# Channel attention into a rational feed-forward layer: a new table of times for the planner, batch 0's sums and the weight conversion on VectorE, the softmax division folded into the split of the fused weights, and three of eight denominators as a product

## The chip, the cores and the metric

The kernel runs on one core of a Trainium2 chip. The time is that of one launch in device microseconds, the median of a few runs. The profile shows one further execution by engine: PE is TensorE (matrix products), DVE is VectorE, ACT is ScalarE, POOL is GpSimd, and SP is SyncE, which here issues every DMA.

## What is computed

```python
# attention over channels, for each of B = 4 batches; q, k, v are [6080, 256]
qn = q / (norm(q, axis=tokens) + 1e-6);  kn = k / (norm(k, axis=tokens) + 1e-6)
s  = kn.T @ qn / tau                       # 256 x 256
a  = exp(s - s.max(-1));  a /= a.sum(-1) + 1e-9
x  = v @ a                                 # 6080 x 256
# a feed-forward layer with a rational activation, over all 24320 tokens
h  = x @ w_in                              # 256 -> 2048
P  = a0 + a1*h + a2*h**2 + a3*h**3
Q  = 1 + abs(b0)*abs(h) + abs(b1)*h**2
out = (P / (Q + 1e-6)) @ w_out             # 2048 -> 256
```

All arrays are float32, except that w_in and w_out reach the kernel as pairs of 32-bit words (float64), from which it forms float32 itself.

## The kernel before

**Tiles and loops.** Tokens are taken in groups of 512 (`GT`); 12 groups make a batch, the last with 448 tokens. The 2048 hidden channels are taken in eight *pairs* of 2 x 128 channels. A pair (`pair`) works on a tile of 128 x 1024 numbers: 12 matmuls fill it in PSUM (`mm1`, into a buffer `hx`), the activation is computed on it, and 8 matmuls by w_out add it to the group's output `acc` (`mm2`, in two steps). In the trace an f32 matmul leaves two records, so `mm2` has 16 records for a pair and `mm1`, in another number format, has 12.

**Attention ahead of time.** `x @ w_in` is not computed in two steps. For each batch, `Attn` streams q and k (24 halves of a group, a buffer `kq` each), lets PE add up k.T @ q, and squares both on ACT (`sq`) for the norms. `softmax` turns this into `ex`, `shares` divides it by its sums (`inverse`), `turned` transposes it into `eT`, and `fuse` multiplies it by w_in: PE writes a tile, ACT copies it to a rounded part `whi`, and DVE forms the rest `wlo`. So `mm1` needs only v: `values` transposes a group of v on PE (into `hx`), and splits it in the same way into `vhi` and `vlo`. Batch b+1's attention runs under batch b's pairs; that of batch 0 stands at the start of the program with nothing to run under.

**Weights.** `piece` makes float32 of 16 pieces (8 of w_in, 8 of w_out), each with an Abs on ACT, five DVE instructions (`low_bits`, `high_bits`, `power`, `low_word`, `cut_off`) and an addition on POOL (`together`).

**A pair's activation.** ACT: Square(h) into `d`, Abs(b0*h) into `kk`, a3*h+a2 into `y`, Abs_reciprocal_sqrt of `d` into `r`, and its Square. POOL: `d = b1*d + 1`, `d += kk`, and later `d = d*r` for one step that refines the quotient. DVE: two steps of P's Horner scheme in `hx`, its product with `r`, and the last step, which writes `g`, the operand of `mm2`.

**What sets the order.** Every piece of work is a `step` with an engine, a cost and a key. The `Planner` plays the steps through with these costs and hands out buffers; on each engine it picks the ready step with the lowest key. The order that comes out is written down, and every engine then runs its instructions strictly in that order. `SLOTS` gives the buffers of each kind: three `hx` (PSUM) are shared by the pairs' tiles, the scores, the transposes and the fused weights, so an `hx` comes free only when its last reader, mostly DVE's last step of a pair, is done. There are also four `d`, four `g`, three `r` and two `sq`.

Of the kernel before, what the change touches and what calls it, by code (L numbers as in the profile page):

```python
# [16 lines left out]
PSUM = bass.MemoryType.PSUM  # L17

# [32 lines left out]
class Step:  # L51
    __slots__ = ("eng", "cost", "fn", "key", "need", "after", "new", "bufs", "banks", "n")


class Planner:

# [8 lines left out]
    def add(self, eng, cost, key, fn, reads=(), writes=()):  # L65
        s = Step()
        s.eng, s.cost, s.fn, s.key = eng, cost, fn, key
        s.n = len(self.steps)
        s.after, s.new, s.bufs = [], [], []
# [26 lines left out]
    def order(self):  # L96
# [26 lines left out]
        while left:  # L123
            for e in ready:
                while busy[e] <= now and ready[e]:
# [17 lines left out]
                    busy[e] = now + pick.cost  # L143
                    for b in pick.banks:
                        b.owner, b.until = e, busy[e] + self.HOP[e]
# [23 lines left out]
def tile_channel_attention_rational_ffn(  # L169
# [15 lines left out]
    P = 128  # L185
# [9 lines left out]
    while n0 < N:  # L195
# [7 lines left out]
    LINE = ("POOL",) * NFP  # L203
# [7 lines left out]
    SLOTS = {"hx": 3, "acc": 1, "d": 4, "uu": 4, "r": 3, "g": 4, "w": 5, "kq": 3, "sq": 2, "ssq": 1,  # L211
             "vst": 1, "vhi": 2, "vlo": 2, "orow": 2, "sacc": 1, "eT": 1, "n2": 1,
             "s0": 1, "y": 1, "e": 1, "sm": 1}
    plan = Planner(SLOTS, ("d", "uu", "r", "g", "w", "kq", "sq", "vst", "vhi", "vlo", "orow"), ("hx", "acc"))
# [23 lines left out]
    def step(eng, cost, key, fn, reads=(), writes=()):  # L238
# [7 lines left out]
        plan.add(eng, cost, key, run, reads, writes)  # L246
# [17 lines left out]


    edge = ONE**0.5
    root, incline, fold, t0, t1, t2 = (
        const.tile([P, 1], F32, name=x) for x in ("root", "incline", "fold", "t0", "t1", "t2")
    )
    dve.tensor_scalar_max(t0, b1, 1e-30)  # L270
    act.activation(t1, t0, AF.Abs_reciprocal_sqrt)
    dve.tensor_tensor(root, t0, t1, op=ALU.mult)
    dve.tensor_tensor(t2, root, root, op=ALU.mult)
    dve.tensor_tensor(t2, t0, t2, op=ALU.subtract)
    dve.scalar_tensor_tensor(t2, t2, 0.5, t1, op0=ALU.mult, op1=ALU.mult)
    dve.tensor_tensor(root, root, t2, op=ALU.add)
    dve.scalar_tensor_tensor(incline, root, -2.0 * edge, b0, op0=ALU.mult, op1=ALU.add)
    dve.tensor_scalar_mul(fold, b0, -2.0)

# [5 lines left out]
    II = 3.5  # L285
    T0 = 80.0
# [3 lines left out]
    def piece(side, m, at, late):  # L290
# [7 lines left out]
        raw = buf("d", [P, 2 * PIECE], U32, "raw")  # L298
        keep = buf("uu", [P, PIECE], F32, "keep")
        top = buf("g", [P, PIECE], U32, "top")  # L300
        unit = buf("r", [P, PIECE], U32, "unit")
# [12 lines left out]
        def low_bits():  # L314
            dve.tensor_scalar(top.tile, hi(), 3, 0x3FFFFFF8, op0=ALU.logical_shift_left, op1=ALU.bitwise_and)

        def high_bits():

            dve.scalar_tensor_tensor(
                top.tile, hi(), 0xC0000000, top.tile, op0=ALU.bitwise_and, op1=ALU.bitwise_or  # L320
            )

        def power():
            dve.tensor_scalar(unit.tile, top.tile, 0xFF800000, None, op0=ALU.bitwise_and)
# [22 lines left out]
        step("DVE", 0.75, c + 2, power, [top], [unit])
        step("DVE", 0.7, c + 3, low_word, [raw, unit], [unit])
        step("POOL", 1.3, c + 4, together, [top, unit], [unit])
        if side == "in":  # L350
            step("DVE", 1.4, c + 5, lambda: cut_off(w_in_sb[:, j, cols]), [keep, unit], [w_in_ok[part, j]])
        else:
            dst = w_out_sb[:, 2 * m : 2 * m + 2].rearrange("p f e -> p (f e)")
            step("DVE", 1.1, c + 5, lambda: cut_off(dst), [keep, unit], [w_out_ok[m]])


    class Attn:


        def __init__(self, b, begin, pace, end):  # L360
            self.b = b
            self.ssq = {}
# [3 lines left out]
            for i in range(2 * NG):  # L366
                self.half(i, begin + i * pace, begin + (i + 1 - i % 2) * pace, sps, "POOL" if not first or i % 3 == 2 else "DVE")
# [3 lines left out]
        def half(self, i, at, both, sps, eng):  # L371
# [12 lines left out]
            step("SP", 1.4, at - (0 if first else 2 * II), load, (), [kq])  # L384

            if half == 0:
                self.slot = sps or buf("hx", [P, 2, GT], F32, "sps")
            slot = self.slot

            def products():  # L390
                for t in range(T // 2):
                    for c in range(NC2):
                        pe.matmul(
                            slot[:, 0, c * C : (c + 1) * C],
                            kq[:pn, t, 0, c * P : (c + 1) * P],
                            kq[:pn, t, 1, :],
                            start=(t == 0 and c == 0 and half == 0 and (g == 0 or not first)),
                            stop=(t == T // 2 - 1 and half == 1 and (g == NG - 1 or not first)),
                            skip_group_check=True,
                        )  # L400

            joined = half == 1 or (first and g > 0)
            step("PE", 1.75, both, products, [kq, slot] if joined else [kq], [slot])
            if half == 1 and not first:
# [7 lines left out]
            if eng not in self.ssq:  # L412
                sq = self.ssq[eng] = buf("orow" if eng == "DVE" else "ssq", [P, 2 * 2 * C], F32, "ssq")
                step("ACT", 1.05, at, lambda: act.activation(sq[:pn], src[1](), AF.Square), [kq], [sq])
            else:
                sq, total = buf("sq", [P, 2 * 2 * C], F32), self.ssq[eng]
                step("ACT", 1.05, at, lambda: act.activation(sq[:pn], src[1](), AF.Square), [kq], [sq])
                e = pool if eng == "POOL" else dve
                step(
                    eng, 2.42 if eng == "POOL" else 1.4, at + 2,  # L420
                    lambda: e.tensor_tensor(total[:pn], sq[:pn], total[:pn], op=ALU.add), [sq, total], [total],
                )

        def softmax(self, at):
# [5 lines left out]
            sums = list(self.ssq.values())  # L430

            def norms_pe():
                parts = [(s, h) for s in sums for h in range(T // 2)]
                for n, (s, h) in enumerate(parts):
                    end = n == len(parts) - 1
                    row = s[:, h * 2 * C : (h + 1) * 2 * C]
                    pe.matmul(
                        nps[:, 0, 0:C], ones, row[:, C : 2 * C], start=(n == 0), stop=end, skip_group_check=True
                    )
                    for i in range(NC2):  # L440
                        pe.matmul(
                            nps[:, 0, C + i : C + i + 1], row[:, i * P : (i + 1) * P], ones[:, 0:1],
                            start=False, stop=end, skip_group_check=True,
                        )

            step("PE", 2.0 * len(sums), at, norms_pe, sums, [nps])
# [12 lines left out]
            step("DVE", 6.5, at + 4, norms_y, [n2, s0], [y, e])  # L459
# [29 lines left out]
            step("ACT", 4.0, at + 10, exps, [sn, stat], [ex, stat])  # L489
# [5 lines left out]
            step("DVE", 0.5, at + 12, inverse, [stat], [stat])  # L495

            def shares():
                for i in range(NC2):
                    act.activation(
                        ex[:, i, :], ex[:, i, :], AF.Identity, scale=stat[:, 3 * NC2 + i : 3 * NC2 + i + 1]  # L500
                    )

            step("ACT", 1.0, at + 13, shares, [ex, stat], [ex])
# [10 lines left out]
            step("PE", 0.7, at + 14, turned, [ex], [eps])  # L514
            fn = lambda: act.copy(eT.tile.rearrange("p j i -> p (j i)"), eps[:, 0, :])
            step("ACT", 0.6, at + 13, fn, [eps], [eT])
            self.w = [self.fuse(j, at + 16 + 2 * II * j, eT) for j in range(NFP // 2)]

        def fuse(self, j, at, eT):

            slot = buf("hx", [P, 2, GT], F32, "fused")
            hi = buf("w", [P, 2, NC2, 2 * P], F32R, "whi")
# [142 lines left out]
    for n, m in enumerate(range(8)):  # L665
        piece("in", m, 8.0 + 4.0 * n, 6.0)
# [52 lines left out]
```

## Time and profile before

| | |
|---|---|
| median of 3 runs | 2801.58 us (2799.64 to 2801.61) |
| profiled execution: its time, its span | 2800.71 us, 2798.9 us |
| busy: PE, DVE, ACT, POOL | 96%, 74%, 77%, 87% of the span |
| first `mm1` starts at | 132.41 us |
| first group's output copied at | 213.9 us |
| group of 512 without attention beside it | 50.9 us |
| moved by DMA | 110 MB, 90% of the DMA engines' time in the first 70.6 us |

Times are microseconds from the span's start. A row of the timeline has start, duration, engine, line, operation, output<-inputs with their shapes, and in brackets how long the engine stood idle before it and for whom. Line 30 is the helper through which all instructions are issued, so rows are told apart by their tiles. The rows of a table by stretches have, for each engine, busy time and (x) instructions, then the granted PE clock as a share, the share of DMA time, and GB/s. In the chain of waits a row has start, length, engine and tile, and the number of instructions.

### The profile page before, as it was taken

How to read it: one execution, taken by the hardware profiler on the slowest of the kernel's cores; microseconds unless marked ns; L12 is line 12 of the kernel's file. 1: busy time of each engine (PE TensorE's matmuls, PEld its weight loads, DVE VectorE, ACT ScalarE, POOL GpSimd, SP SyncE). 2: the span in 40 equal slices, each digit the busy share in tenths (PEclk: the TensorE clock that was granted, in tenths of full speed). 3: DMA queues.
4: the chain of work that ended last, by engine and by line, in shares of the span. 5: the costliest groups of instructions: out<-in, count | busy, mean ns of one | idle time of the engine just before them, and what ended most of it. 6: DMA issues, size and time to landing. Idle time of an engine off the chain costs nothing.

```text
span 2798.9 us, 32559 instructions
## 1 busy us (share of the span) xinstructions
PE 2689.2 (96%) x12236; PEld 2280.4 (81%) x12236; DVE 2075.6 (74%) x1800; ACT 2157.4 (77%) x2188; POOL 2432.9 (87%) x1251
## 2 busy tenths in 40 slices
PE   7489999999999999999999999999999999999999
PEld 6468888888788888888878888888887888888887
DVE  7687777777767777777776777777777677777776
ACT  4378888787777878887786787878777788888886
POOL 3489999999779999999887999999896799999997
PEclk9699999999999999999999999999999999999999
DMA  9300111110000101010100111111100000000000
GB/s 289 93 8 31 31 38 44 49 36 29 31 30 31 46 31 61 31 46 30 59 15 15 45 36 56 31 46 34 47 16 16 15 31 16 16 31 16 30 8 15
DMA packets 69326, 110.11 MB, mean 39 GB/s; under 512 B 5296, under 2 KB 53936, under 8 KB 69168
## 3 DMA queue, kind: packets, MB, share of 16 engines
q1 hardware_dynamic: 69168, 108.03, 12.0%
q8 instruction: 96, 1.57, 0.2%
q14 instruction: 62, 0.51, 0.1%
HBM read 83.10 MB, written 24.90 MB: 39 GB/s over the span
## 4 chain that ended last, share of the span: by engine, by line
PE 57%; POOL 22%; ACT 8%; DVE 5%; issue 5%; DMA 1%; SPq 0%; ACTq 0%; POOLq 0%; DVEq 0%
PE acc L30 28%; PE hx L30 28%; POOL d L30 21%; ACT uu L30 3%; ACT r L30 2%; ACT d L30 2%; POOL ssq L30 2%; DVE g L30 2%; DMA kq<-in_q_dram 1%; DVE hx L30 1%; ACT orow L30 0%; DVE w_out_sb L30 0%; DVE sq L30 0%; DVE r L30 0%; DVE y L30 0%
## 5 line engine op out<-in xcount | busy, mean ns | idle before, releaser
L30 PE MATMUL acc<-w_out_sb,g 128*128 128x256 f32 (+1 forms) x6144 | 1384.5, 379 | 9.7 <-ACT orow L30 8.4
L30 PEld LDWEIGHTS acc<-w_out_sb,g 128*128 128x128 f32 (+1 forms) x6144 | 1155.9, 189 | 182.6 <-ACT orow L30 11.7
L30 PE MATMUL hx<-vhi,w 128*128 128x512 f32 (+1 forms) x3072 | 1047.5, 407 | 39.8 <-DVE g L30 32.5
L30 POOL TENSOR_TENSOR d<-d,r 128x1024 f32<-128x1024 f32 (+1 forms) x384 | 903.8, 2360 | 89.4 <-ACT r L30 88.7
L30 POOL TENSOR_TENSOR d<-d,uu 128x1024 f32<-128x1024 f32 (+1 forms) x384 | 908.0, 2365 | 32.2 <-POOL d L30 0.3
L30 DVE TENSOR_TENSOR uu<-uu,hx 128x1024 f32<-128x1024 f32 (+1 forms) x384 | 463.4, 1207 | 392.3 <-ACT uu L30 391.7
L30 PEld LDWEIGHTS hx<-vhi,w 128*128 128x128 f32 x3072 | 581.9, 189 | 179.3 <-DVE g L30 41.2
L30 ACT ACTIVATE d<-hx 128x1024 f32<-128x1024 f32 (+1 forms) x384 | 388.6, 1012 | 295.0 <-PE hx L30 293.9
L30 PE MATMUL hx<-vlo,w 128*128 128x512 f32 (+1 forms) x1536 | 598.9, 390 | 0.0
L30 DVE SCALAR_TENSOR_TENSOR g<-d,hx 128x1024 f32<-128x1024 f32 (+1 forms) x384 | 462.8, 1206 | 154.2 <-POOL d L30 142.5
L30 ACT ACTIVATE r<-d 128x1024 f32<-128x1024 f32 (+1 forms) x384 | 405.6, 1056 | 203.6 <-POOL d L30 201.8
L30 POOL TENSOR_SCALAR d<-d,babs 128x1024 f32<-128x1024 f32 (+1 forms) x384 | 429.4, 1118 | 144.8 <-ACT d L30 144.1
L30 DVE SCALAR_TENSOR_TENSOR hx<-hx,coef,r 128x1024 f32<-128x1024 f32 (+1 forms) x384 | 489.9, 1276 | 76.4 <-ACT r L30 76.2
L30 DVE SCALAR_TENSOR_TENSOR hx<-uu,coef,hx 128x1024 f32<-128x1024 f32 (+1 forms) x384 | 488.6, 1272 | 6.1
L30 ACT ACTIVATE uu<-hx,coef 128x1024 f32<-128x1024 f32 (+1 forms) x384 | 462.2, 1204 | 0.2 <-DVE w_out_sb L30 0.2
L30 ACT ACTIVATE uu<-hx,babs 128x1024 f32<-128x1024 f32 (+1 forms) x384 | 425.0, 1107 | 1.4 <-PE hx L30 1.4
L30 ACT ACTIVATE r<-r 128x1024 f32<-128x1024 f32 (+1 forms) x384 | 406.1, 1057 | 5.0
L30 PEld LDWEIGHTS hx<-vlo,w 128*128 128x128 f32 x1536 | 291.8, 190 | 55.0
L30 POOL TENSOR_TENSOR ssq<-sq,ssq 128x1024 f32<-128x1024 f32 (+1 forms) x76 | 183.7, 2417 | 49.1 <-ACT sq L30 48.4
L30 PE MATMUL hx<-kq 128*128 128x256 f32 (+1 forms) x672 | 157.8, 390 | 11.5 <-DMA kq<-in_q_dram 6.9
L30 PEld LDWEIGHTS hx<-kq 128*128 128x128 f32 (+1 forms) x672 | 130.9, 196 | 32.8 <-DMA kq<-in_k_dram 6.9
L30 ACT ACTIVATE sq<-kq 128x1024 f32<-128x1024 f32 (+1 forms) x79 | 82.4, 1058 | 53.6 <-DMA kq<-in_q_dram 36.4
(71 smaller groups left out, 724.9 us busy)
## 6 DMA issues: line engine op xcount, KB each, us to landing
vst<-in_v_dram SPq DMA_DIRECT2D x44, 512.0 KB, 3.6
out_dram<-orow SPq DMA_DIRECT2D x44, 512.0 KB, 2.7
kq<-in_k_dram SPq DMA_DIRECT2D x78, 256.0 KB, 3.6
kq<-in_q_dram SPq DMA_DIRECT2D x78, 256.0 KB, 4.0
d<-in_moe_w_in_dram SPq DMA_DIRECT2D x8, 512.0 KB, 5.8
d<-in_moe_w_out_dram SPq DMA_DIRECT2D x8, 512.0 KB, 3.6
r<-in_k_dram SPq DMA_DIRECT2D x10, 256.0 KB, 5.7
r<-in_q_dram SPq DMA_DIRECT2D x10, 256.0 KB, 5.9
```

The costliest lines, as they stand in the source:

```text
L30: ins = op(*args, **kwargs)
```

## The change

- Order: `TIME` and `LAG` give the keys of all stages; the start of the pairs has key 52.18 (80 before), and a pair's steps have other distances. The planner also learns that some DVE steps and all POOL steps exclude each other (`port`).
- Start: v's group 1 is loaded only after the first `whi` (`gate`). Batch 0's squares are all summed on DVE (`orow`; before, a third of them went to POOL). Four pieces of w_in are converted early; four others and all of w_out come later, in buffers of their own (`cv`, `cv2`) with their raw words in `kq` (four of them now), and `together` moves from POOL to DVE. A DVE step `fold` halves the sum before the norms' matmuls, of which 3 are left for each batch (before: 12 for batch 0, 6 for the others).
- Softmax: `shares` is gone. `fuse` works on one pair's weights (8 tiles for a batch, before 4 of double size); ACT multiplies by 1/sum while it writes `whi`, as two instructions of 128 x 256, and DVE does so while it writes `wlo`, also as two.
- Attention: both halves of a group are multiplied in one step. Batch 1's 24 halves follow at 0.95 pairs each (before 3.4), those of batches 2 and 3 at 2.7.
- Denominator: from the second group on, pairs 1, 5 and 7 (`FACTORED`) form Q - 1 as h*(b1*abs(h) + b0) with an Abs, a DVE product and another Abs; the one is added as the bias of the root on ACT, and by a POOL instruction for the later product. This has five ACT, five DVE and two POOL instructions, where the other pairs have five, four and three.

```diff
+LAG = {
+    "first": 3.38, "prod": 6.03, "abs": -6.89, "line": 2.25, "second": 4.09, "sum": -5.43, "slope": 5.2,
...
+TIME = {
+    "pair": 3.54, "start": 52.18, "load": 2.03, "softmax": 48.33, "in": 9.33, "late_in": 4.0, "out0": 1.98,
...
-    SLOTS = {"hx": 3, "acc": 1, "d": 4, "uu": 4, "r": 3, "g": 4, "w": 5, "kq": 3, "sq": 2, "ssq": 1,
+    SLOTS = {"hx": 3, "acc": 1, "d": 4, "uu": 4, "r": 3, "g": 4, "w": 10, "kq": 4, "sq": 2, "ssq": 1,
...
-        raw = buf("d", [P, 2 * PIECE], U32, "raw")
+        early = side == "in" and m < 4
+        raw = buf("d" if early else "kq", [P, 2 * PIECE], U32, "raw")
+        work = buf("uu" if early else "cv", [P, 2, PIECE], F32, "work")
+        unit = buf("r" if early else "cv2", [P, PIECE], U32, "unit")
...
-            pool.tensor_tensor(rest, rest, top.tile.bitcast(F32), op=ALU.add)
+            dve.tensor_tensor(rest, rest, top(F32), op=ALU.add)
...
-                e = pool if eng == "POOL" else dve
+                e = dve if first else pool
...
+            def fold():
+                dve.tensor_tensor(total[:, : 2 * C], total[:, : 2 * C], total[:, 2 * C :], op=ALU.add)
...
-                    act.activation(
-                        ex[:, i, :], ex[:, i, :], AF.Identity, scale=stat[:, 3 * NC2 + i : 3 * NC2 + i + 1]
-                    )
...
+                    act.activation(hi[:, i, :], src, AF.Identity, scale=share)
...
+                    dve.scalar_tensor_tensor(
+                        lo[:, i, :], src, share, hi[:, i, :].bitcast(F32), op0=ALU.mult, op1=ALU.subtract
+                    )
...
+        if m >= NFP and p in FACTORED:
+            fn = lambda: act.activation(c(kk), c(hx), AF.Abs, scale=b1)
+            fn = lambda: dve.scalar_tensor_tensor(c(d), c(kk), b0, c(hx), op0=ALU.add, op1=ALU.mult)
+            fn = lambda: act.activation(c(d), c(d), AF.Abs)
...
+        more = ONE if m >= NFP and p in FACTORED else 0.0
+        fn = lambda: act.activation(c(r), c(d), AF.Abs_reciprocal_sqrt, bias=more)
+        if m >= NFP and p in FACTORED:
+            fn = lambda: pool.tensor_scalar(c(d), c(d), ONE, None, op0=ALU.add)
...
+    gate = [attns[0].w[0][0]]
```

**PE between batch 0's norms and the first pair.** Before; `ident,vst` is the transposition of v's group 1, `ident,sq` is `turned`, `w_in_sb,eT` is `fuse`, `kq` is k.T @ q:

```order
L30 MATMUL hx_112<-ones,ssq_121 128x1 x2
L30 MATMUL hx_112<-ident,vst_138 128x128 x8
L30 MATMUL hx_111<-kq_116 128x256 x4
L30 MATMUL hx_111<-kq_114 128x256 x4
L30 MATMUL hx_112<-ident,sq_119 128x128 x4
L30 MATMUL hx_113<-kq_115 128x256 x4
L30 MATMUL hx_111<-w_in_sb,eT_127 128x256 x8
L30 MATMUL hx_112<-w_in_sb,eT_127 128x256 x8
L30 MATMUL hx_113<-kq_116 128x256 x4
L30 MATMUL hx_111<-vhi_139,w_128 128x512
```

Now:

```order
L43 MATMUL hx_101<-ones,orow_102 128x1 x2
L43 MATMUL hx_100<-kq_93 128x256 x4
L43 MATMUL hx_100<-kq_92 128x256 x4
L43 MATMUL hx_101<-ident,sq_105 128x128 x4
L43 MATMUL hx_99<-w_in_sb,eT_111 128x256 x4
L43 MATMUL hx_100<-w_in_sb,eT_111 128x256 x4
L43 MATMUL hx_101<-kq_92 128x256 x4
L43 MATMUL hx_101<-kq_94 128x256 x4
L43 MATMUL hx_99<-vhi_133,w_112 128x512
```

Before, `turned` went into the `hx` in which v's group 1 had just been transposed; now it goes into that of the norms, and v's group 1 comes after the first two pairs.

**DVE at the same place.** Before, the reader of that `hx` (`vlo`) stood here, behind the conversion of w_out:

```order
L30 SCALAR_TENSOR_TENSOR g_105<-d_97,g_105 128x512
L30 SCALAR_TENSOR_TENSOR w_out_sb<-uu_100,r_108 128x512
L30 TENSOR_SCALAR r_109<-g_105 128x512
L30 SCALAR_TENSOR_TENSOR r_109<-d_97,r_109 128x512
L30 TENSOR_TENSOR vlo_142<-hx_112,vhi_140 128x1024
L30 COPY sacc_143<-hx_113 128x512
L30 TENSOR_TENSOR sacc_143<-hx_111,sacc_143 128x512
L30 TENSOR_TENSOR w_133<-hx_111,w_128 128x1024
```

Now the first two `wlo` stand between pieces, and conversions go on between the first group's pairs:

```order
L43 SCALAR_TENSOR_TENSOR w_in_sb<-cv_96,cv_98 128x512
L43 TENSOR_SCALAR cv_97<-kq_93 128x512
L43 SCALAR_TENSOR_TENSOR cv_97<-kq_93,cv_97 128x512
L43 SCALAR_TENSOR_TENSOR w_122<-hx_99,sm_110,w_112 128x256 x2
L43 SCALAR_TENSOR_TENSOR w_123<-hx_100,sm_110,w_113 128x256 x2
L43 TENSOR_SCALAR cv_98<-cv_97 128x512
L43 TENSOR_TENSOR sacc_137<-hx_101,sacc_137 128x512
L43 SCALAR_TENSOR_TENSOR cv_98<-kq_93,cv_98 128x512
```

Before, three pieces of w_out were converted between the softmax and this `vlo`. Now the conversion is spread: 28 of its instructions stand between the second `wlo` and the first group's last `g`.

**POOL in a group without attention.** Before, every pair had three rows:

```order
L30 TENSOR_SCALAR d_97<-d_97,babs 128x1024
L30 TENSOR_TENSOR d_97<-d_97,uu_102 128x1024
L30 TENSOR_TENSOR d_96<-d_96,r_110 128x1024
L30 TENSOR_SCALAR d_99<-d_99,babs 128x1024
L30 TENSOR_TENSOR d_99<-d_99,uu_101 128x1024
L30 TENSOR_TENSOR d_97<-d_97,r_108 128x1024
```

Now a pair of `FACTORED` (here `d_84` and `d_82`) has two, without the addition of `uu`:

```order
L43 TENSOR_SCALAR d_84<-d_84 128x1024
L43 TENSOR_TENSOR d_84<-d_84,r_91 128x1024
L43 TENSOR_SCALAR d_81<-d_81,babs 128x1024
L43 TENSOR_TENSOR d_81<-d_81,uu_85 128x1024
L43 TENSOR_TENSOR d_81<-d_81,r_90 128x1024
L43 TENSOR_SCALAR d_82<-d_82 128x1024
L43 TENSOR_TENSOR d_82<-d_82,r_89 128x1024
```

More of the change, by code (lines that the diff above doesn't have):

```diff
@@ L51 @@
 class Step:
-    __slots__ = ("eng", "cost", "fn", "key", "need", "after", "new", "bufs", "banks", "n")
+    __slots__ = ("eng", "cost", "fn", "key", "need", "after", "new", "bufs", "banks", "port", "n")
 class Planner:
@@ L107, in order @@
         events, out, now = [], [], 0.0
+        port = {"DVE": 0.0, "POOL": 0.0}
         for s in self.steps:
@@ L143, in order @@
                     busy[e] = now + pick.cost
+                    if pick.port:
+                        other = "POOL" if e == "DVE" else "DVE"
+                        busy[e] = max(now, port[other]) + pick.cost
+                        port[e] = busy[e]
                     for b in pick.banks:
@@ L201, in tile_channel_attention_rational_ffn @@
     TG = B * NG
-    LINE = ("POOL",) * NFP
+    FACTORED = (1, 5, 7)
     pe = InOrder(tc, nc.tensor)
@@ L244, in run @@
             fn()
-        plan.add(eng, cost, key, run, reads, writes)
+        plan.add(eng, cost, key, run, reads, writes, port)
     ident = const.tile([P, P], F32, name="ident")
@@ L284, in tile_channel_attention_rational_ffn, with piece @@
     PIECE = 512
-    II = 3.5
-    T0 = 80.0
+    II = TIME["pair"]
+    T0 = TIME["start"]
     w_in_ok = {(part, j): Buf() for part in range(4) for j in range(NC2)}
     w_out_ok = [Buf() for _ in range(NFP)]
-    def piece(side, m, at, late):
+    def piece(side, m, at, c):
         if side == "in":
@@ L366, in __init__, with half @@
             for i in range(2 * NG):
-                self.half(i, begin + i * pace, begin + (i + 1 - i % 2) * pace, sps, "POOL" if not first or i % 3 == 2 else "DVE")
+                both = begin + (i if first else i + 1 - i % 2) * pace
+                self.half(i, begin + i * pace, both, sps)
             self.scores = sps if first else self.sacc
             self.softmax(end)
-        def half(self, i, at, both, sps, eng):
+        def half(self, i, at, both, sps):
             g, half = divmod(i, 2)
@@ L382, in load @@
                     sp.dma_start(kq[:pn, :, j, :], rows[:, half * T // 2 : (half + 1) * T // 2, :])
[L384 to L404, printed above, removed]
+            step("SP", 1.4, at - (0 if first else 2 * II), load, self.gate, [kq])
+            self.kq[half] = kq
+            if first:
+                fn = lambda: self.products(sps, [kq], pn, i == 0, i == 2 * NG - 1)
+                step("PE", 1.75, both, fn, [kq, sps] if i else [kq], [sps])
+            elif half == 1:
+                pair, slot = list(self.kq), buf("hx", [P, 2, GT], F32, "sps")
+                step("PE", 3.5, both, lambda: self.products(slot, pair, pn, True, True), pair, [slot])
                 if g == 0:
@@ L521, in fuse @@
+        def fuse(self, p, at, eT, stat):
             slot = buf("hx", [P, 2, GT], F32, "fused")
[L522 to L535 removed]
@@ new lines, in fuse, with part @@
+            lo = buf("w2", [P, NC2, 2 * P], F32R, "wlo")
+            cols = slice(2 * p * P, 2 * (p + 1) * P)
+            def part(i):
+                return slot[:, 0, i * 256 : (i + 1) * 256], stat[:, 3 * NC2 + i : 3 * NC2 + i + 1]
+            def products():
+                for i in range(NC2):
+                    for c in range(NC2):
+                        pe.matmul(
+                            part(i)[0], eT[:, c, i * P : (i + 1) * P], w_in_sb[:, c, cols],
+                            start=(i == 0 and c == 0), stop=(c == NC2 - 1), skip_group_check=True,
+                        )
```

231 lines of the change are left out of this document (103 added, 128 removed).

## The prediction

> **What bounds the kernel now.** I read the page first, then busy time by stretches (the groups' ends as borders), the chain of waits in a plain group, and the timeline at the start and at a softmax.
>
> ```profile
> span 2798.9 us, 32559 instructions
> PE 2689.2 (96%) x12236; PEld 2280.4 (81%) x12236; DVE 2075.6 (74%) x1800; ACT 2157.4 (77%) x2188; POOL 2432.9 (87%) x1251
> ...
> core 0: us, PE busy (x) PEld busy (x) DVE busy (x) ACT busy (x) POOL busy (x), PEclk, DMA share, GB/s
> 0.00:70.60 70.60, 52.03 (x216) 43.54 (x216) 52.39 (x55) 34.37 (x38) 27.56 (x20) 0.95 0.90 289
> 70.60:132.41 61.81, 26.95 (x101) 22.91 (x101) 45.16 (x59) 18.04 (x24) 29.85 (x17) 0.64 0.28 85
> 132.41:213.90 81.49, 70.53 (x296) 57.88 (x295) 65.85 (x55) 59.51 (x61) 65.81 (x34) 0.94 0.06 20
> 315.70:703.40 387.70, 383.61 (x1754) 325.54 (x1753) 283.95 (x240) 310.63 (x310) 362.52 (x184) 1.00 0.13 41
> 833.60:1384.50 550.90, 543.70 (x2482) 461.11 (x2481) 402.84 (x340) 441.78 (x440) 513.40 (x260) 1.00 0.13 40
> 1384.50:1448.90 64.40, 57.93 (x267) 49.89 (x266) 50.84 (x50) 48.47 (x56) 48.53 (x26) 0.95 0.11 33
> 2346.10:2397.00 50.90, 50.87 (x234) 42.94 (x233) 39.55 (x34) 42.03 (x43) 46.87 (x25) 1.00 0.06 22
> ```
>
> The last row is a group of batch 3, with no attention beside it: PE is busy 50.87 of 50.90 us. That is the floor, and the change does not touch it: a group keeps its matmuls. The chain of waits in such a group is made of PE alone, and gives the price of a pair's `mm1` (12 records) and `mm2` (16 records):
>
> ```profile
> 2342.32 3.45 PE acc L30 x16
> ...
> 2354.78 2.76 PE hx L30 x12
> ```
>
> So a pair costs PE 6.2 us, a record of `mm1` 0.23 us, any other f32 record of 256 columns 0.216 us. What can be won is PE's idle time: the start (until 213.9 us), about 6.5 us at a softmax (row 1384.5; there are three such stretches), and 4.1 + 7.2 + 7.2 us in the groups with attention (rows 315.7, 833.6; the third, in batch 2, repeats the second).
>
> **The start up to the first pair.** Before, the last sum of squares ends on POOL at 70.6 us, and the first `mm1` starts 62 us later:
>
> ```profile
> 67.78 2.83 POOL L30 TENSOR_TENSOR ssq<-sq,ssq 112x1024 f32<-112x1024 f32 x1 [6.03 <-ACT sq L30]
> ...
> 114.31 2.78 POOL L30 TENSOR_TENSOR ssq<-sq,ssq 128x1024 f32<-128x1024 f32 x1
> 114.82 2.82 DVE L30 SCALAR_TENSOR_TENSOR w_out_sb<-uu,r 128x512 f32<-128x512 f32 x1
> ...
> 118.62 1.22 DVE L30 TENSOR_TENSOR vlo<-hx,vhi 128x1024 fp32r<-128x1024 f32 x1
> 119.99 1.09 PE L30 MATMUL hx<-ident,sq 128*128 128x128 f32 x4 [21.88 <-DVE vlo L30]
> ...
> 132.41 0.58 PE L30 MATMUL hx<-vhi,w 128*128 128x512 f32 x1
> ```
>
> PE stands 21.88 us before `turned`, since its `hx` is held until `vlo`, which DVE reaches only behind the conversion; and the conversion is slow, since an instruction between SBUF tiles takes 2.82 us while POOL works, against 0.68 and 0.42 us where POOL is idle:
>
> ```profile
> 9.45 1.23 DVE L30 TENSOR_TENSOR orow<-sq,orow 128x1024 f32<-128x1024 f32 x1 [2.46 <-ACT sq L30]
> 16.24 2.56 DVE L30 TENSOR_SCALAR g<-d 128x512 uint32<-128x512 uint32 x1 [0.39 <-DMA d<-in_moe_w_in_dram]
> 22.97 0.42 DVE L30 TENSOR_SCALAR g<-d 128x512 uint32<-128x512 uint32 x1
> 29.85 0.68 DVE L30 SCALAR_TENSOR_TENSOR w_in_sb<-uu,r 128x512 f32<-128x512 f32 x1
> ```
>
> In the new order POOL has nothing until batch 1's squares, so the sums and pieces run at the short prices. A piece is then 0.42 + 0.68 + 0.42 + 0.68 + 0.62 (`together`, half of 1.23) + 0.68 = 3.5 us. Up to its last sum DVE has 23 sums x 1.23, seven pieces x 3.5 and a `vlo` of 1.22: 54 us, from 9.45 us on, so 63.5 us, and some 4 us of waits at the first loads: 68 us. The loads are not later: 33 transfers of 0.52 MB up to batch 0's last half make 17.3 MB, 60 us at the 289 GB/s of the first stretch; the two w_out and w_in pieces ahead of that half on SP's queue wait for `kq` tiles that DVE frees by 50 us.
>
> From 68 us DVE has, up to the scores' maximum, `fold` 0.6, the norms (2.6 of small steps, 1.9 of reciprocals), the scores 1.7, and 16 instructions of pieces at 9.3: 16 us. Then exps 1.4 and `turned` 1.1 (slow clock), `eT` 0.6, the first weights' 8 records at half speed 3.4, the second's 1.7, four halves of batch 1 at 0.216 x 16 = 3.5 for the two that stand ahead: 12 us. DVE's way to the first `wlo` (13 instructions, 7 us) and its 0.95 us fit under that. First `mm1` at 68 + 28 = 96 us, 36 us earlier. PE's work done by then shrinks: before 64.5 us (24 halves 41.5, six of batch 1 10.4, norms 3.5, transposes 2.2, four weights 6.9), now 54.1 (41.5, four halves 6.9, 0.9, 1.3, two weights 3.5). Of the difference of 10.4, 2.6 are norms that are gone; 8 us come later. **Term: -36 + 8 = -28 us.** Bounds: the sums end at 66 or 72, and POOL's first three additions for batch 1 may stop DVE for up to 3 x 2.4 us: -34 to -17.
>
> The loads of w_out that move behind the start meet idle DMA engines (share 0.28, then 0.06). The new wait, group 1's v behind the first `whi`, lets it land some 4 us later (the row below), while PE has two `mm1` (5.5 us) ahead of its transposition: nothing.
>
> ```profile
> vst<-in_v_dram SPq DMA_DIRECT2D x44, 512.0 KB, 3.6
> ```
>
> **The first group.** Before it lasts 81.5 us for 296 records, about 67.5 us of PE work; 14 us are lost. Now PE has eight pairs' `mm2` 27.6, eleven `mm1` 30.3, six weights 10.4, eight halves 13.8, a transposition 0.9: 83 us. DVE has more:
>
> ```profile
> L30 DVE SCALAR_TENSOR_TENSOR hx<-hx,coef,r 128x1024 f32<-128x1024 f32 x10 | 12.8, 1284 | 1.4 <-ACT r L30 1.4
> L30 DVE SCALAR_TENSOR_TENSOR hx<-uu,coef,hx 128x1024 f32<-128x1024 f32 x10 | 12.8, 1281 | 0.1
> L30 DVE TENSOR_TENSOR uu<-uu,hx 128x1024 f32<-128x1024 f32 x10 | 12.2, 1215 | 12.6 <-ACT uu L30 12.6
> L30 DVE SCALAR_TENSOR_TENSOR g<-d,hx 128x1024 f32<-128x1024 f32 x10 | 12.1, 1213 | 0.3
> L30 DVE SCALAR_TENSOR_TENSOR w_out_sb<-uu,r 128x512 f32<-128x512 f32 x3 | 6.3, 2096 | 1.1 <-POOL r L30 1.1
> ...
> L30 DVE TENSOR_SCALAR r<-g 128x512 uint32<-128x512 uint32 x2 | 3.5, 1733 | 0.0
> ```
>
> These are DVE's groups in 132 to 214 us. Eight pairs x 5.0 = 40; 28 instructions of pieces, 16.6 us at the short prices, and a wait for POOL on each: the eleven of before took 15.8 us instead of 6.5, 0.85 each, so 24 us; seven `wlo` x 0.95, a `vlo`, four additions of scores (0.69): 10. Sum 91 us from about 93 us on, so the last `g` comes at 184 at the earliest, with waits for ACT and POOL near 190, and PE's end of the group near 194: 98 us, of which 15 are lost, as before. **Term: 0.** Bounds: PE alone sets the time (-14), or every one of the 28 waits for a whole POOL instruction of 2.39 us: (2.39 - 0.85) x 28 = +43.
>
> ```profile
> L30 POOL TENSOR_TENSOR d<-d,uu 128x1024 f32<-128x1024 f32 x352 | 840.9, 2389 | 29.6 <-POOL d L30 0.3
> ```
>
> A wait on DVE holds the pairs behind it, and through `g` PE; that is why the price of the lock counts here and nowhere else.
>
> **The three later softmaxes.** Before, DVE works 16.2 us from one `g` to the next, PE waits 6.19 us, and then runs 12 matmuls in 4.5 us that take 2.4 (7/8 of 2.76) elsewhere:
>
> ```profile
> 1416.06 1.22 DVE L30 SCALAR_TENSOR_TENSOR g<-d,hx 128x1024 f32<-128x1024 f32 x1 [0.80 <-POOL d L30]
> ...
> 1426.81 3.56 DVE L30 SCALAR_TENSOR_TENSOR sq<-sacc,n,y 128x256 f32<-128x256 f32 x2
> ...
> 1432.24 1.21 DVE L30 SCALAR_TENSOR_TENSOR g<-d,hx 128x1024 f32<-128x1024 f32 x1
> ...
> 1433.50 0.74 PE L30 MATMUL hx<-vhi,w 128*128 128x448 f32 x1 [6.19 <-DVE g L30]
> ...
> 1434.42 0.95 PE L30 MATMUL hx<-vhi,w 128*128 128x448 f32 x2
> ...
> 153.79 0.50 PE L30 MATMUL hx<-vhi,w 128*128 128x512 f32 x1 [2.40 <-DVE g L30]
> ...
> 154.37 1.05 PE L30 MATMUL hx<-vhi,w 128*128 128x512 f32 x2
> ```
>
> The new order puts a `g` in the middle: by the same durations 10.4 us, then 11.7 us, and PE holds half a pair of `mm2` more in reserve (1.7 us). The softmax's own work on DVE is not less. Between no gain and all of 6.2 us I take a wait of 3 us, and half of the slow clock, since at 153.79 us even 2.40 us of idleness are followed by matmuls at 0.42 us. That is 3.2 + 1.0 for each of the three. **Term: -13 us** (0 to -25). The Trainium skill, page "TensorE: Matmul & The Clock Gate", section "What's actually happening", lets the clock fall only after an idle window of about 3.4 us; by that rule a 3 us wait would cost no slow clock and the term would be -16. The row at 153.79 us speaks against relying on it.
>
> **Groups with attention.** 18.5 us are idle in their 27 groups, mostly for `g`. POOL gives up an addition of 2.39 us in three of eight pairs, ACT keeps its five instructions, DVE gains a product of 1.28 (row `hx<-uu,coef,hx`) and stays at 40 + 4 of 51 us. Batch 1's faster halves cost PE only what they cost anyway: two additions' time of POOL for a pair, 5 + 2.5 us, stays under PE's 8. **Term: -7 us** (0 to -16). The norms of three batches lose 3 of 6 matmuls: **-3 us**. The split of the weights adds 2.3 us to ACT and to DVE for a batch, under PE's fuse work; nothing.
>
> **Sum.** 2798.9 - 28 + 0 - 13 - 7 - 3 = 2748 us of span; with 1.8 us around it (2800.71 - 2798.9), and 0.9 us that the median of the runs lies above that execution, 2750 us.
>
> **Rivals.**
> - *PE alone bounds the first group and the softmaxes leave no wait.* For it: POOL idles during the sums, and the order is drawn with the exclusion in view. Against it: 91 us of DVE against 83. 2750 - 14 - 12 = 2724.
> - *The lock decides.* Every piece's instruction in the first group waits for a whole POOL instruction: 2750 + 43 = 2793. The row of 2.096 us speaks for it, the mean of 0.85 us against it. The Trainium skill, page "SBUF — State Buffer", section "Who interferes with whom", says that a DVE instruction with two SBUF inputs excludes a GpSimd instruction that reads SBUF; by that rule moving `together` to DVE adds such instructions.
> - *Slower: the `hx` come back too late in every group.* The new PE order of a plain group fills three `hx` in a row, then 20 matmuls of `mm2`, so three tiles of eight must be back 14.1 us after their `mm1` (2 x 2.75 + 40 x 0.216); before it was 15.9. The trace shows 12.3 us:
>
> ```profile
> 2348.32 0.40 PE L30 MATMUL hx<-vhi,w 128*128 128x512 f32 x1
> ...
> 2359.82 1.22 DVE L30 SCALAR_TENSOR_TENSOR g<-d,hx 128x1024 f32<-128x1024 f32 x1
> ```
>
> From 14.5 us on (0.36 us x 3 x 47 groups = 51) the gain is gone; at 15.0 us it costs 127 us: 2877. Against it: the margin is 1.8 us and a tile of `FACTORED` saves POOL's addition.
>
> **Chances.** My forecast 0.67, PE alone 0.17, the lock 0.10, late `hx` 0.06. The range takes the bounds of the start and softmax terms and the second case whole: 2714 to 2790. 0.2% (5.6 us) is about what a measurement of this kernel tells from no change. Faster: 0.67 + 0.17 + half of the lock's case, 0.89; same 0.05; slower 0.06.
>
> **What would show it.** First `mm1` near 96 us and `turned` without a long wait; the first group's end near 194 us; 50.9 us for a plain group (52 or more there would prove the late `hx`); PE waits of about 3 us at the softmaxes; POOL near 75% of the span (2433 us less 141 additions of 2.39 and the sums of batch 0). A first `mm1` after 110 us, or conversion rows of 2.8 us throughout the first group, would make the forecast wrong.

## The result: 2.9% slower, and the profile after

The changed kernel takes 2882.1 us (median; 2880.8 to 2883.8) against 2801.6 us before: 1.0288 times as long, with a 95% interval of 1.0270 to 1.0306. The page's head gives the profiled execution:

```profile
span 2879.3 us, 32475 instructions
PE 2704.5 (94%) x12200; PEld 2277.3 (79%) x12200; DVE 2251.5 (78%) x2009; ACT 2187.3 (76%) x2227; POOL 2288.8 (79%) x1087
```

PE has fewer instructions, and POOL 144 us less work than before. The span grew all the same, so the time must be in waits. The same stretches as in the prediction show where (up to the last sum of squares; to the first `mm1`; the first group; a group with nothing beside it; the group with the next batch's softmax):

```profile
core 0: us, PE busy (x) PEld busy (x) DVE busy (x) ACT busy (x) POOL busy (x), PEclk, DMA share, GB/s
0.00:72.40 72.40, 48.27 (x190) 40.15 (x191) 53.32 (x67) 34.47 (x37) 0.83 (x7) 0.86 0.82 259
72.40:104.86 32.46, 20.38 (x69) 15.47 (x69) 26.79 (x48) 11.51 (x19) 7.41 (x3) 0.74 0.37 116
104.86:210.00 105.14, 90.53 (x390) 75.74 (x389) 91.17 (x87) 73.37 (x82) 84.33 (x40) 0.92 0.26 80
618.00:672.80 54.80, 51.11 (x233) 42.91 (x232) 43.14 (x37) 42.66 (x42) 44.50 (x21) 1.00 0.05 19
779.60:849.40 69.80, 63.28 (x286) 53.04 (x287) 55.24 (x64) 50.35 (x65) 47.69 (x24) 0.98 0.02 8
```

The first group ends at 210.0 us instead of 213.9. But a plain group takes 54.8 us here (53.7 to 55.4 in the last batch) instead of 50.9, with POOL at 44.5 us of work and DVE at 43.1, neither of them full. The groups of POOL's instructions hold the cause:

```profile
L43 POOL TENSOR_TENSOR d<-d,r 128x1024 f32<-128x1024 f32 x352 | 836.0, 2380 | 244.6 <-ACT r L43 237.9
L43 POOL TENSOR_TENSOR d<-d,uu 128x1024 f32<-128x1024 f32 x223 | 532.8, 2389 | 16.4 <-ACT uu L43 0.5
L43 POOL TENSOR_SCALAR d<-d 128x1024 f32<-128x1024 f32 x129 | 357.8, 2774 | 85.9 <-ACT r L43 76.6 <-DVE uu L43 9.2
L43 POOL TENSOR_SCALAR d<-d,babs 128x1024 f32<-128x1024 f32 x223 | 252.0, 1130 | 59.0 <-ACT d L43 58.8
```

The two `TENSOR_SCALAR` groups have the same engine, shape and type. The one with `babs` (times b1, plus ONE) takes 1.13 us; the new one (plus ONE alone) takes 2.77 us, more than an addition of two tiles. The planner's table has 1.13 for both. In the timeline of a plain group one sees what that does:

```profile
631.57 2.78 POOL L43 TENSOR_SCALAR d<-d 128x1024 f32<-128x1024 f32 x1
634.31 2.40 POOL L43 TENSOR_TENSOR d<-d,uu 128x1024 f32<-128x1024 f32 x1
636.74 1.06 ACT L43 ACTIVATE r<-d 128x1024 f32<-128x1024 f32 x1 [2.90 <-POOL d L43]
638.92 1.29 DVE L43 SCALAR_TENSOR_TENSOR hx<-hx,coef,r 128x1024 f32<-128x1024 f32 x1 [2.38 <-ACT r L43]
641.39 0.50 PE L43 MATMUL hx<-vhi,w 128*128 128x512 f32 x1 [0.42 <-DVE g L43]
...
644.81 2.77 POOL L43 TENSOR_SCALAR d<-d 128x1024 f32<-128x1024 f32 x1 [3.41 <-ACT r L43]
...
653.63 1.06 ACT L43 ACTIVATE r<-d 128x1024 f32<-128x1024 f32 x1 [2.71 <-POOL d L43]
...
658.33 1.22 DVE L43 SCALAR_TENSOR_TENSOR g<-d,hx 128x1024 f32<-128x1024 f32 x1
659.61 0.50 PE L43 MATMUL hx<-vhi,w 128*128 128x512 f32 x1 [1.11 <-DVE g L43]
...
668.23 1.09 PE L43 MATMUL hx<-ident,vst 128*128 128x128 f32 x8 [2.15 <-DVE g L43]
```

At 631.57 the long addition holds back the sum of another tile behind it on POOL; ACT's root waits 2.90 us for that sum, and everything behind the root on ACT waits too. DVE waits for the root, and PE for `g`. The tile whose `mm1` starts at 641.39 comes back with the `g` that ends at 659.55, and the next `mm1` into that `hx` starts right then, 1.11 us late. The largest wait of the group, 2.15 us, stands ahead of the transposition of v, which takes an `hx` too and waits for the next `g`. With the 0.42 us at 641.39 these three make 3.7 us. POOL is idle elsewhere in the group; that time is of no use, since POOL then waits for ACT, which had waited for POOL.

The table of waits says it for the whole span. PE's waits for `g` grew from 34.2 us in 27 places to:

```profile
PE hx L43 <- DVE g L43: 111.2, 87, 9.8
```

For comparisons between kernels I count PE's work as each kind's number of matmuls times the median distance between their starts; what is left of the time up to the last group's end is idle. By that count the changed kernel has 2632 us of work and 242.4 idle, the kernel before 2648 and 146.

### The profile page after: what moved, and what is told of

The parts are those of the page before. It is cut to its first block, busy times and chain, and to the rows that moved or that the text cites. A ratio compares the mean times of both kernels' runs of the same rounds, so it can differ in the third digit from the quotient of the medians.

```text
span 2879.3 us, 32475 instructions
## 1 busy us (share of the span) xinstructions
PE 2704.5 (94%) x12200; PEld 2277.3 (79%) x12200; DVE 2251.5 (78%) x2009; ACT 2187.3 (76%) x2227; POOL 2288.8 (79%) x1087
## 4 chain that ended last, share of the span: by engine, by line
PE 38%; POOL 25%; ACT 20%; issue 9%; DVE 7%; DMA 1%; SPq 0%; POOLq 0%; DVEq 0%; ACTq 0%
POOL d L43 24%; PE hx L43 20%; PE acc L43 18%; ACT r L43 9%; ACT uu L43 6%; ACT d L43 3%; DVE g L43 2%; POOL ssq L43 2%; DVE d L43 1%; DVE hx L43 1%; DMA kq<-in_q_dram 1%; DVE e L43 0%; DMA r<-in_q_dram 0%; DVE uu L43 0%; ACT sq L43 0%
## 5 line engine op out<-in xcount | busy, mean ns | idle before, releaser
L43 PE MATMUL hx<-vhi,w 128*128 128x512 f32 (+1 forms) x3072 | 1034.9, 404 | 60.4 <-DVE g L43 39.9
L43 POOL TENSOR_TENSOR d<-d,uu 128x1024 f32<-128x1024 f32 (+1 forms) x243 | 574.8, 2366 | 17.9 <-ACT uu L43 0.5
L43 POOL TENSOR_SCALAR d<-d 128x1024 f32<-128x1024 f32 (+1 forms) x141 | 387.3, 2746 | 93.1 <-ACT r L43 83.5
L43 ACT ACTIVATE d<-hx 128x1024 f32<-128x1024 f32 (+1 forms) x243 | 244.8, 1007 | 149.4 <-PE hx L43 146.0
L43 POOL TENSOR_SCALAR d<-d,babs 128x1024 f32<-128x1024 f32 (+1 forms) x243 | 272.3, 1121 | 80.2 <-ACT d L43 80.1
L43 POOL TENSOR_TENSOR ssq<-sq,ssq 128x1024 f32<-128x1024 f32 (+1 forms) x69 | 165.6, 2400 | 116.8 <-ACT sq L43 110.7
L43 DVE SCALAR_TENSOR_TENSOR d<-uu,babs,hx 128x1024 f32<-128x1024 f32 (+1 forms) x141 | 178.2, 1264 | 34.8 <-ACT uu L43 31.7
```

Source lines behind the costliest of these rows:

```text
L43: ins = op(*args, **kwargs)
```

## The experiments

Theory A: the price of POOL's one-operation addition is the cause. Theory B, the rival: the new lags fill three `hx` in a row and leave too little time, whatever POOL costs. Theory C: the product's own longer way (Abs, product, Abs, root) is late.

**The addition in another form (e1_two_op).** The column `ones` makes it a multiplication and an addition. The values are the same, and so is the order on every engine.

```
-            fn = lambda: pool.tensor_scalar(c(d), c(d), ONE, None, op0=ALU.add)
+            fn = lambda: pool.tensor_scalar(c(d), c(d), ones[:, 0:1], ONE, op0=ALU.mult, op1=ALU.add)
```

> The added instruction alone is written in another form (times a column of ones, plus ONE, as two operations with a pointer, like the line with babs beside it); all engines keep the order of the changed kernel, instruction by instruction. Theory A (the price of the one-operation form, 2.77 us where the plan put 1.13, makes g late in every group): the instruction takes about 1.13 us, a plain group falls from 54.8 to 51 us, PE's idle time outside the first group from 170 us to about 65, the whole to 2740-2785 us. Theory B (three mm1 in a row leave too little time for hx to come back, whatever POOL costs): the instruction falls too, but the plain group stays at 53.5 us or more and the whole above 2850. Theory C (the longer way of a product, Abs, product, Abs, root, is what is late): half of it comes back, 2810-2850.

It took 2727.5 us: 0.9733 of the time before (0.9719 to 0.9748), and 154.6 us less than the changed kernel. From its groups, its stretches (two plain groups) and its table of waits:

```profile
L43 POOL TENSOR_SCALAR d<-d,ones 128x1024 f32<-128x1024 f32 x129 | 145.6, 1129 | 95.6 <-ACT r L43 84.8 <-DVE uu L43 10.6
```

```profile
435.10:485.50 50.40, 50.40 (x234) 43.16 (x233) 43.21 (x37) 42.88 (x43) 39.74 (x22) 1.00 0.06 22
...
2334.80:2385.20 50.40, 50.40 (x234) 43.18 (x233) 43.34 (x37) 42.91 (x44) 39.87 (x23) 1.00 0.06 22
```

```profile
PE hx L43 <- DVE g L43: 15.0, 7, 9.8
```

PE's work is the same 2632 us; its idle time falls from 242.4 to 87.8 us, which is the whole difference of 155. A plain group of 54.8 us loses 4.4 of the 4.9 us that three instructions had too much (3 x 1.64); in the last batch it is 3.3 to 5.0. DVE's busy time is the same in both kernels (2251.5 and 2254.8 us), so the long instruction does not act by making DVE's instructions longer. With nothing else moved, theory A is shown and B and C have nothing left to explain. The time is 12 us below what A expected, since a plain group went to 50.4 us and not only to 51. The same place in the order, from the timeline of a plain group:

```profile
2354.49 0.58 PE L43 MATMUL hx<-vhi,w 128*128 128x512 f32 x1
...
2368.17 1.21 DVE L43 SCALAR_TENSOR_TENSOR g<-d,hx 128x1024 f32<-128x1024 f32 x1
...
2371.31 0.58 PE L43 MATMUL hx<-vhi,w 128*128 128x512 f32 x1
```

`g` ends 1.9 us before PE comes back for the `hx`: 13.7 us lie between the end of the one `mm1` (2357.58) and the start of the other, and 11.8 are needed. In the changed kernel the tile at 641.39 needed 15.1.

**Which forms are slow (e2_forms, e9_forms).** Each of the three product tiles gets its own form. In e9_forms tile 5 leaves the addition out and tile 1 adds 0.0 behind it; only the instructions' durations are read there.

```
 e2_forms                                                  e9_forms
 p=1: (d, 1.0, ONE, op0=mult, op1=add)                     (d, ONE, 0.0, op0=add, op1=add)
 p=5: (d, lift, None, op0=add)   # lift: a column of ONE   (d, ONE, None, op0=mult)
 p=7: (d, ONE, None, op0=add)                              (d, ONE, 1.0, op0=add, op1=mult)
```

> The price of POOL's addition of ONE in three forms within one run: tile 1 of the product tiles uses two operations with two immediates, tile 5 one operation with a pointer to a column that holds ONE, tile 7 the form of the changed kernel. If the number of operations decides: 1.13, 2.77, 2.77 us. If the kind of operand decides (an immediate as first scalar is slow): 2.77, 1.13, 2.77. If it takes two operations and a pointer: 2.77 for all three. Time between 2740 and 2885 accordingly.

> Three further forms of POOL's instruction in one run: tile 1 adds ONE and then 0.0 (two operations, both additions), tile 5 multiplies by ONE in one operation (its addition is left out), tile 7 adds ONE and multiplies by 1.0. If a second operation is what makes the instruction quick: 1.1, 2.77, 1.1 us. If an addition as the first operation is slow: 2.77, 1.1, 2.77 us. If only multiply-then-add is quick: 2.77 us for all three.

POOL's rows in the timelines of e2_forms (tiles 7, 1 and 5) and of e9_forms (tiles 1, 5 and 7):

```profile
248.37 2.76 POOL L43 TENSOR_SCALAR d<-d 128x1024 f32<-128x1024 f32 x1
...
268.86 1.07 POOL L43 TENSOR_SCALAR d<-d 128x1024 f32<-128x1024 f32 x1
...
294.14 2.85 POOL L43 TENSOR_SCALAR d<-d,lift 128x1024 f32<-128x1024 f32 x1
```

```profile
203.99 3.64 POOL L43 TENSOR_SCALAR d<-d 128x1024 f32<-128x1024 f32 x1
...
237.65 2.80 POOL L43 TENSOR_SCALAR d<-d 128x1024 f32<-128x1024 f32 x1
...
253.23 1.07 POOL L43 TENSOR_SCALAR d<-d 128x1024 f32<-128x1024 f32 x1
```

The first run said that the number of operations decides, not the kind of operand. The second refuted that as well: two additions take 3.64 us, and a single multiplication is as slow as a single addition. Of seven forms (those of `babs` and `ones`, a column and then an immediate, count as one), the quick ones are those with one multiplication and one addition, in either order, with immediates or a pointer: 1.05 to 1.13 us. Why is not shown. The two times, 2823.4 and 2863.2 us (one run each), lie between the quick and the slow kernel: e2_forms, with two slow instructions in a group, stands 96 us above 2727.5, the changed kernel, with three, 155.

**No product at all (e3_no_product), and the planner told the true price (e4_true_price).**

```
e3:  FACTORED = ()
e4:  step("POOL", 2.78 * s, at + LAG["one"], fn, [d], [d])      # was 1.13 * s
```

> No tile computes its denominator as a product: FACTORED is empty, so the slow instruction is gone, and also the product's longer way; head, tables and planner stay as changed. Theory A: 2740-2785 us (PE's work 2631, the first group's 71 idle, some 60 elsewhere, 5 behind the end), plain groups near 51. Theory B (the new lags are too tight by themselves): plain groups at 53 or more, above 2840. Theory C: like A, and clearly below the two-operation form.

> The changed kernel with one number of the planner set right: the addition of ONE is entered with 2.78 us instead of 1.13, the instruction itself stays. Theory A, if the fixed order around the slow instruction is the trouble and not POOL's sum of work (44.5 us in a group of 51): a good part comes back, 2770-2840 us. If the longer instruction on the way from ACT's root to g is the trouble wherever it stands: 2850-2885. Theory B: unchanged, 2865-2890.

e3 took 2798.4 us (0.9987, 0.9977 to 0.9996), plain groups 51.2; e4 took 2816.9 (1.0054, 1.0039 to 1.0069), plain groups 52.7. e4 is what theory A expects if a good part of the harm comes from an order drawn with a wrong price: 65 of 155 us return with one number. The rest stays, though POOL is busy only 44.6 of 52.7 us. e3 missed what A expected by 13 us, and there theory A says nothing: without the product the new lags gain almost nothing. That left open what head, lags and product are worth apart.

**Head, lags and product apart (e5, e7, e8).** *Head* stands here for all of the change but the lags and the product: start, softmax, split of the weights, planner. e5 puts the two-operation product into `pair()` of the kernel before, with the lags written there. e7 and e8 are the changed kernel with those lags of before, without a product and with the two-operation one. First the lags of e7 and e8, then the product in e5 (shortened):

```
+LAG = {"first": 2.7, "prod": 4.0, "abs": 5.3, "line": 3.8, "second": 3.9, "sum": 6.0, "slope": 5.1, "num1": 6.4, "num2": 7.7,
+       "root": 8.4, "one": 9.3, "square": 9.5, "again": 10.7, "quot": 10.7, "last": 13.0, "out": 15.0}      # "finish": 11.0
```

```
+        product = m >= NFP and p in (1, 5, 7)
+        if product:
+            step("ACT", 1.12 * s, at + 2.7, ...)    # kk = Abs(b1 * hx)
+            step("DVE", 1.28 * s, at + 4.0, ...)    # d = (kk + b0) * hx
+            step("ACT", 1.02 * s, at + 5.3, ...)    # d = Abs(d)
...
+            step("POOL", 1.13 * s, at + 9.3, ...)   # d = d * ones + ONE, behind the root with bias ONE
```

> The kernel before with one part of the change: tiles 1, 5 and 7 of every group but the first get the denominator as a product, with the addition of ONE in two operations (1.13 us); head, planner and the lags written into pair() stay as before. If POOL's relief (three additions of 2.39 us in a group, 87% busy) is what the two-operation kernel gains outside the first group, and any order will do: PE's idle time there falls from 64 us to 20-30, 2750-2775 us. If the product needs lags made for it (Abs, product, Abs is a longer way to the root): 2785-2830 us.

> The changed kernel with no product and with the lags of the kernel before: only head, softmaxes, split of the fused weights and planner are new. By the terms of the prediction (start 28 us, softmaxes 13, norms 3): 2750-2765 us, first mm1 near 105, first group's end near 196. If the body's order decides more than the head (the run without products and with the new lags gave 2798): 2785-2800 us, first group's end above 200, PE waits of 5 us and more left at the softmaxes.

> The changed kernel with the two-operation addition and with the lags of the kernel before. If the lags matter little once POOL is relieved: 2722-2740 us. If the new lags carry a part of the gain: 2750-2800 us, plain groups at 50.9 us or more instead of 50.4. Theory B (the new lags harm) would put it below 2720.

**The slow form elsewhere (e6, e10).** e5 and e8 with the one-operation addition of the changed kernel:

```
-pool.tensor_scalar(c(d), c(d), ones[:, 0:1], ONE, op0=ALU.mult, op1=ALU.add)
+pool.tensor_scalar(c(d), c(d), ONE, None, op0=ALU.add)
```

> The kernel before with the product in tiles 1, 5 and 7 and with the changed kernel's one-operation addition (2.77 us) instead of the two-operation one, which gave 2785.7 here. POOL's work in a group still falls, by 0.75 us a product tile. If only POOL's sum of work counts: no harm, 2785-2800. If the longer instruction delays g wherever it stands, by as much as in the changed kernel (155 us for 141 instructions, 1.1 us of the added 1.64 each): 2920-2950. If the lags of before leave it room: 2800-2860.

> The changed kernel as it is, one-operation addition included, with the lags of the kernel before; the two-operation form gave 2760.8 there. If the slow instruction costs what it does with the new lags (155 us): 2900-2930. If the harm comes only from the new lags, which were made for 1.13 us, and the old ones have room: 2765-2800. Between: 2800-2860.

The medians in us side by side, with the ratios to the kernel before (intervals all within 0.002 either way):

| | no product | product, two operations | product, one operation |
|---|---|---|---|
| head and lags of before | 2802 | 2785.7 (0.9939) | 2951.0 (1.0535) |
| new head, lags of before | 2774.6 (0.9898) | 2760.8 (0.9850) | 2940.8 (1.0491) |
| new head, new lags | 2798.4 (0.9987) | 2727.5 (0.9733) | 2882.1 (1.0288) |

Read along the rows: the one-operation form costs 165, 180 and 155 us, wherever it stands; in e6 and e10 that is at and above the upper end of what was expected. The new lags do not make it worse, they soften it, so theory B is wrong also in the sense that looser lags would have helped. That only POOL's sum of work counts is refuted: in e6 POOL works 44.65 us of a plain group, less than the 46.9 before, and the group still takes 4.3 us longer.

```profile
2516.40:2571.60 55.20, 51.22 (x234) 42.93 (x233) 43.19 (x36) 42.68 (x44) 44.65 (x22) 1.00 0.05 20
```

Read down the columns: the new lags cost 24 us without products and bring 33 with quick ones. They fit the product and the product fits them; the lags of before leave most of POOL's relief unused (e5: 17 us). The head alone brings 28 us, between the two expectations of e7; why the new lags cost 24 us without products was not looked into.

**A fourth product tile (e11_four).** `FACTORED = (1, 3, 5, 7)` in the two-operation kernel.

> The two-operation kernel (2727.5) with a fourth product tile, 3. PE waits only 16 us outside the first group there, so at most some 10 us can come; DVE gets 1.28 us more in each group and POOL 1.25 less. If POOL still decides at the softmaxes: 2718-2727. If the extra product disturbs the order or DVE becomes the bound (46 of 50.4 us): 2730-2760.

2738.4 us (0.9767, 0.9751 to 0.9783), 11 us more than with three: POOL falls to 37.4 us in a plain group, DVE rises to 44.4, and PE's idle time outside the first group grows from 16 to 29 us. So e1_two_op is the best version found.

## Why the prediction was wrong, step by step

- **The step that failed** is the price of an instruction that I never wrote down. In "Groups with attention" I let POOL "give up an addition of 2.39 us" and said nothing of the addition of ONE that a product tile gets; silently it stood at the price of the row beside it, 1.13 us, as in the planner's table. No row of before shows a one-operation `TENSOR_SCALAR` on POOL. It took 2.77 us, and that alone is 155 us of the time; with the silent price (e1_two_op) the kernel takes 2727.5 us, inside the range. It should have been bounded from both sides like other unseen operations: 1.13 us by the `babs` row, 2.39 by the addition of two tiles. Even that upper end lies below the measured 2.77, but it would have brought the slow case in sight: by the three rows of the table, known only afterwards, 141 such instructions cost 155 to 180 us for an added 1.64 each, that is 1.1 to 1.3 us each, or 0.67 to 0.78 us for each us added, so 1.26 us more would have cost 120 to 140 us and turned the sign. The Trainium skill, page "GPSIMD Engine Reference", section "4.1 Engine selection", calls operations with one input on this engine roughly line-rate; the quick forms agree (1.07 us for 1024 elements), the one-operation forms at 2.8 us do not, and the measurement decides.
- **The late `hx`.** The rival named the wait that came, with the right length (a return at 15.0 us; 15.1 for the tile above), but not its cause: it blamed the new order, and in e1_two_op the same order leaves 1.9 us to spare. That its 2877 us lie so close to 2882 is partly luck: it put 127 us on top of 2750, and measured are 155 on top of 2727.5. I gave it 0.06, because the margin in the trace of before was 1.8 us. That margin was read with the durations of before. 1.64 us more in each POOL addition of ONE, on a way that POOL and ACT pass to each other, used it up.
- **The rest of the sum** can be read from e1_two_op, where that instruction has the price I had assumed: 74 us below before in span, where I had 51. That the two lie only 23 us apart is luck in part: the start brought 15 us less than I had put, the other terms 38 us more. The terms came out like this. *The start* (-28): the first `mm1` comes at 104.8 us instead of 96, and the first group loses 21 us instead of 15 (103.7 us for 82.7 of work); its idle time, start included, falls from 82 to 72 us, and with the first batch's norms the term is -13. In the changed kernel the last sum ends at 72.4 instead of 68 (the row at 72.42 is `fold`, right behind it): DVE's work up to there is 53 us, as summed, but from its first sum on it stands still for 9 us, most of it waiting for squares, where I had some 4. Then loads of batch 1 that the new order has put ahead of `turned` hold up both PE (5.78 us) and ACT, which squares the same half ahead of the exps; and the exps (`sq<-sq,sm`) wait a last 1.16 us for POOL's sum of that half. When PE is through with the half, `turned` still waits 0.39 us for them:

```profile
72.42 0.69 DVE L43 TENSOR_TENSOR orow<-orow 128x512 f32<-128x512 f32 x1
...
88.11 1.06 ACT L43 ACTIVATE sq<-kq 128x1024 f32<-128x1024 f32 x1 [2.56 <-DMA kq<-in_q_dram]
88.15 3.75 PE L43 MATMUL hx<-kq 128*128 128x256 f32 x8 [5.78 <-DMA kq<-in_q_dram]
...
89.26 2.34 POOL L43 TENSOR_TENSOR ssq<-sq,ssq 128x1024 f32<-128x1024 f32 x1 [87.82 <-ACT sq L43]
91.63 0.51 ACT L43 ACTIVATE sq<-sq,sm 128x256 f32<-128x256 f32 x1 [1.16 <-POOL ssq L43]
...
92.29 1.39 PE L43 MATMUL hx<-ident,sq 128*128 128x128 f32 x4 [0.39 <-ACT sq L43]
95.98 5.78 PE L43 MATMUL hx<-w_in_sb,eT 128*128 128x256 f32 x16 [2.30 <-ACT eT L43]
...
104.86 0.58 PE L43 MATMUL hx<-vhi,w 128*128 128x512 f32 x1
```

- *The softmaxes* (-13): the three stretches lose 12 us instead of 28 in e1_two_op, -15; in e7, the head without the products, they still lose 28. So the new order of the softmax alone, to which I gave the gain, did nothing. With the products but the lags of before (e8) the loss is 26 us, with the new lags but no products (e3) 25, so the new head needs both. In e5, with the old head and the old order of the softmax, the products alone bring the loss to 14 us; that the new order has any part in the -15 is therefore not shown. *Groups with attention* (-7): all groups but the first and those three stretches lose 4 us instead of 36, so this was the term that was most too small. I had called PE's 50.87 busy of 50.90 us in a plain group "the floor". It is not: 234 matmul records of the same kinds take 50.40 us in e1_two_op. The modelled ends of matmuls covered waits of about 0.3 and 0.4 us ahead of two `mm1`, which only the distances of the starts show. *Norms* (-3): the remaining 14 us are PE's work by my count, norms with 36 matmul records fewer (8 us, of which 2.6 stand in the start) and records of `mm1` with `vhi` at 0.227 instead of 0.230 us (2816 of them, 8.5 us by the medians). In a plain group these records take 15.6 us in sum before and 15.7 in e1_two_op, so the 8.5 us belong to covered waits too.
- **The slow clock.** I did not rely on the Trainium skill's rule (page "TensorE: Matmul & The Clock Gate", section "What's actually happening"), by which an idle window of about 3.4 us is needed. Two waits at the same place, in e1_two_op and in the changed kernel:

```profile
740.13 0.47 PE L43 MATMUL hx<-vhi,w 128*128 128x448 f32 x1 [3.31 <-DVE vlo L43]
...
782.93 0.74 PE L43 MATMUL hx<-vhi,w 128*128 128x448 f32 x1 [4.44 <-DVE vlo L43]
```

The first is followed by full speed, the second by half (a granted clock of 0.50 from 782.86 us on). But the length of a wait does not decide: in e7 a wait of 3.06 us (748.73 to 751.79 us) was followed by half speed. The granted clock tells more. It changes in all these traces only at steps of 3.41 us, so I set the stretches to those steps; first two of e1_two_op, then two of e7:

```profile
735.05:738.46 3.41, 1.77 (x9) 1.21 (x7) 3.34 (x3) 2.81 (x4) 2.61 (x2) 1.00 0.26 106
738.46:741.87 3.41, 1.74 (x9) 1.63 (x10) 3.27 (x5) 0.00 (x0) 0.00 (x0) 1.00 0.38 154
...
749.82:753.23 3.41, 1.44 (x7) 1.35 (x8) 3.38 (x5) 0.00 (x0) 0.03 (x1) 1.00 0.02 5
753.23:756.65 3.42, 2.24 (x8) 1.45 (x6) 3.42 (x6) 1.18 (x2) 0.16 (x1) 0.50 0.00 0
```

The wait of e1_two_op falls half into one step and half into the next, PE works 1.77 and 1.74 us of the two, and the clock stays whole. In e7 one step holds more of the wait, PE works 1.44 us of it, and in the next step the clock is half. My row at 153.79 us fits: its 2.40 us lie in one step (150.93 to 154.34 us) with 1.01 us of PE's work, and the step after it is granted 0.50. So the step is as long as the rule's window, but it need not be wholly idle, and where a wait falls on the steps counts as much as its length. The wait at the softmaxes is now for `vlo`, not for a `g`, as I had thought.
- **The lock** was smaller than I had put it: in the first group (104.9 to 210 us) 27 instructions of pieces took 32.4 us instead of 16.5 at the short prices, 0.59 us of waiting each where I had 0.85. That the group ends at 210 and not at 194 us comes from the later start (9 us) and from 6 us more of idle time on PE.
- **POOL near 75% of the span** is what e1_two_op shows (76%); the 79% of the changed kernel are the 229 us that 141 instructions had too much (129 x 1.64 and 12 x 1.44).

## What to carry to other kernels

Every instruction that a change adds gets a price from a row of its own form, operations counted, not of its name and shape; if there is none, measure it first, since one run with a form for each tile is enough. Where engines in fixed order hand a tile back and forth, an instruction's added length goes to the end even if its engine has a fifth of its time free: here two thirds and more of it. An order drawn from a table of costs should be looked at once against the trace, row by row: here one instruction of 2.77 us, entered with 1.13, turned a gain of 2.7% into a loss of 2.9%, and the right number in the table brought back only 65 of 155 us.

## What the runs showed of the hardware

- POOL's `TENSOR_SCALAR` over 128x1024 f32 between SBUF tiles takes 1.05 to 1.13 us with one multiplication and one addition, in either order, 2.77 to 2.85 us with one operation alone, and 3.64 us with two additions. A lone operation takes longer than a multiplication with an addition; by what mechanism no run here tells.
- A plain group's 234 matmul records need 50.4 us where no wait stands between them; "busy 100%" at 50.9 us was not yet the end.
- The granted clock of PE changed only at steps of 3.41 us, in all 13 traces. Counted over them, 137 steps at full speed had less than 1.4 us of PE's work, and every one was followed by half speed; none with more than 1.83 us was. Between the two both happened.
